# Quarter sums of a DFT matrix in DRAM: eight transfers of 1 MB, or sixteen of 512 KB placed elsewhere

## The chip, the cores and the metric

The kernel runs on one core of a Trainium2 chip. The metric is the device time of one execution in microseconds (us), lower is better; of several timed executions the median is taken.

## What is computed

The reference mixes two branches with a gate per token, all in float32, for 2048 tokens of width 512:

```python
g = sigmoid((x * gate_w).sum(-1, keepdims=True))
a = Cs @ (x @ Cd.T) - Ss @ (x @ Sd.T)      # Real(DFT over tokens of DFT over the width)
b = (silu(x @ w1) * (x @ w3)) @ w2         # SwiGLU, hidden width 1376
out = g * a + (1 - g) * b
```

`Cs`, `Ss` are the real and imaginary 2048x2048 DFT matrices over the tokens (the kernel's input `cc`), `Cd`, `Sd` those of 512x512 over the width (`dd`).

## The kernel before

**Arithmetic.** Every float32 operand is split into a high and a low part (`high`, a copy on ACT, and `low`, a subtraction on DVE), and each product is three matmuls: high by high, high by low, low by high (`mm3`, L124 in the profile). Blocks of 2x2 are multiplied with seven products instead of eight (Strassen-Winograd), so operands are sums of blocks, made on DVE.

**Stages.** In order of time: *gate/up*, L335 to L397, one call `gate_up(n)` per chunk of 128 hidden columns and group of 1024 tokens; then the *transform*, blocks 0 to 3 ("F" blocks, 28 steps each of 12 matmuls, rows of `cc` as the moving operand `zo`); then two blocks of the down projection ("H", moving operand read back from `hsp`), and two of the transform over the width ("Y", from `zsp`). A step loads its operand blocks `B` (`load_c`, L733), sums them on DVE (`sum_c`, L703 and L707), splits them into `zo` (`split_c`, L110 on ACT, L113 on DVE) and multiplies; loads run 8 steps ahead, splits 3. One step of 12 matmuls takes 2.59 us on PE.

**What gate/up moves.** SP loads raw weights `ws` (L224, 512 KB each). ACT and DVE split them to `wa` and, after sums `wu` (L246 to L249), to `wb`. GpSimd's queue (POOL in the profile) stores each `wb` for later use (`wbsp`, L261, 1 MB, two buffers `wb`), and each result `h` in two halves (`hsp`, L324, 256 KB each, three buffers).

**The transform's first block.** Besides the 28 steps, block 0 also loads `xs` (L764, eight of 512 KB), makes from it the second half of the stationary operand (`sum2` on DVE, L178; `high_a2` on ACT, `low_a2` on DVE), and makes the gates: the scores come back from DRAM broadcast to 128 partitions (`s1g<-gs`, L784), ACT applies the sigmoid (L796) and the scalings (L800, L804), and POOL stores them (`gsp`, `ngsp`, L805 and L806). The results of block 0 go to `zsp` by POOL's queue (L933).

**The quarter sums.** The product P1 of blocks 2 and 3 is replaced by one more level of seven products (steps "m1" to "m7", placed among the steps of blocks 1 and 2). Five of them need sums of quarters of `cc`. Four sums are made in DRAM, in the buffer `tsp` of 4 x 2 x 128 x 1024 floats (1 MB for each sum), with no compute engine: a transfer from `cc` (or from an earlier sum) to `tsp`, and an accumulating transfer that adds a second quarter to it. Both go through POOL's queue:

```python
for n, i, b, c in ((0, 1, "b12", "b11"), (1, 3, "b12", "b22"), (2, 2, "T1", "b22"),
                   (3, 4, "T2", "b21")):
    at(0, 3 + 7 * n, quarter_sum, i, b)
    at(0, 6 + 7 * n, lambda i=i, c=c: quarter_sum(i, c, accum_op=ALU.add))
```

`at(blk, n, f)` calls `f` ahead of step `n` of block `blk`, so these eight transfers of 1 MB stand ahead of steps 3, 6, 10, 13, 17, 20, 24 and 27 of block 0. The first read of a sum (`m<-tsp`, L733 on SP) is at 326.1 us.

**What sets the order.** The whole order is written out by hand (`manual_schedule`): each engine and each queue works through its instructions in program order. In gate/up, the tables `early`, `ahead`, `second`, `mid` and `at_end` hold calls for a given `n`; `mid` runs just after the store of `wb`, ahead of the two stores of `h`, and `at_end` after them. An instruction at the head of POOL's queue that waits holds up all behind it.

Of the kernel before, what the change touches and what calls it, by code (L numbers as in the profile page):

```python
# [10 lines left out]
ALU = mybir.AluOpType  # L11
# [22 lines left out]
def fnet_swiglu_gate_kernel(  # L34
# [21 lines left out]
    nc = tc.nc  # L56
# [47 lines left out]
    def free(*tiles):  # L104
        for t in tiles:
            _, places, at = HELD.pop(id(t))
            places.append(at)

    def high(hi, src):
        nc.scalar.activation(hi, src, AF.Copy)  # L110
# [30 lines left out]
    tsp = dram.tile([4, 2, P, 1024], F32, tag="tsp", name="tsp")  # L141
# [63 lines left out]
    def sum_xo(g, k, t):  # L205
        ST[g, k] = t
        nc.vector.tensor_sub(t, *(ST[g, v] for v in SUMS[k]))
# [43 lines left out]
    def wb_parts(w):  # L251
        return flat(WB[w][:, 0]), flat(WB[w][:, 1]), flat(WU[w])

    def high_wb(w):
        WB[w] = wbp.tile([P, 2, 4, 256], F32R, tag="wb", name=f"wb{w}")
        high(wb_parts(w)[0], wb_parts(w)[2])
# [6 lines left out]
    def prod(ps, n, wi, xi, start, chain=False):  # L263
        w = WSET[n]
        w, wi = (WA[w], wi) if wi < 3 else (WB[w], wi - 3)
        x = XO[ITEMS[n][1]]
        for q in range(2):
            sl = slice(q * P, (q + 1) * P)
            mm3(ps, w[:, 0, wi, sl], w[:, 1, wi, sl], x[:, 0, xi, q, :], x[:, 1, xi, q, :],
                start and q == 0, q == 1, chain)  # L270
# [11 lines left out]
    def seed(n, x):  # L282

        y = bank(4 + n % 2, f"Y{n}")
        nc.scalar.activation(y, x, AF.Copy)
        G[n] = (x, y)

    def first2(n):
        prod(G[n][1], n, 1, 1, False, True)
# [26 lines left out]
    def store_h(n, k, h):  # L316

        c, g = ITEMS[n]
        if c == NC - 1:
            nc.gpsimd.dma_start(hlsp[g, :, k * 512 : (k + 1) * 512], h)  # L320
            return
        j = c % NP2
        b = 2 * (c >= NP2)
        nc.gpsimd.dma_start(hsp[g, b + k, j // 2, :, j % 2 * 512 : (j % 2 + 1) * 512], h)  # L324


    early, ahead, second, mid, at_end = {}, {}, {}, {}, {}
# [88 lines left out]
    b12, a21 = zt[0].rearrange("p h a n -> p h (a n)"), zt[1][:, :, 0]  # L416
# [16 lines left out]
    def xo_half(k, q):  # L433
        i = OPS.index(k)
        return XO[0][:, 0, i, q], XO[0][:, 1, i, q], ST[0, k][:, q * 512 : (q + 1) * 512]

    s1 = s1p.tile([P, 512], F32, tag="s1", name="s1_0")
    g1 = u4p.tile([P, 512], F32, tag="u4", name="g1_0")
    h0 = hp.tile([P, 1024], F32, tag="h", name="h0")
# [49 lines left out]
    nc.vector.tensor_mul(h0[:, 512:], g1, C[1, 1])  # L489
    store_h(0, 1, h0[:, 512:])  # L490
    high_wb(1)
    first2(1)
    seed(2, x2)
    low_wb(1)
# [1 line left out]
    gate1(1)  # L496
    sum_xo(0, "T3", ST[0, "B12"])
    sum_xo(0, "T4", ST[0, "B21"])
    first2(2)
    seed(3, x3)  # L500
    for q in range(2):
# [6 lines left out]
    def do(work, n, f, *a):  # L508
        work.setdefault(n, []).append(lambda: f(*a))
# [14 lines left out]
        do(early, n + 3, lambda k=k: low(*xo_parts(1, k)))  # L524
    for n, k in ((7, "B12"), (7, "B11"), (8, "B21"), (9, "B22")):
        do(early, n, lambda k=k: free(ST[1, k]))

    W2R = {}

# [66 lines left out]
    n = NI - 1 - LOOK  # L596
# [35 lines left out]
    for blk, nq in enumerate(NQ):  # L632
        todo_p1 = []
        for n, (k, form, q) in enumerate((k, form, q) for k, form in ORDER[blk] for q in range(nq)):
# [8 lines left out]
            for name in AMONG.get((blk, n), ()):  # L643
                k, h = name[:2], "ab".index(name[2])
# [534 lines left out]
    def at(blk, n, f, *a):  # L1179
        todo.setdefault(NEW[START[blk] + n], []).append((f, a))  # L1180
# [10 lines left out]
    for g, n in enumerate((5, 3)):  # L1191
        for i in range(4):
            at(g, n + i, gates, g, i)
    def quarter_sum(i, b, **kw):


        src = tsp[int(b[1]) - 1] if b[0] == "T" else cc[2 + (b[2] == "2"), 0, 2 * (b[1] == "2") :][:2]
        nc.gpsimd.dma_start(tsp[i - 1], src, max_dma_last_dim=4096, **kw)

    for n, i, b, c in ((0, 1, "b12", "b11"), (1, 3, "b12", "b22"), (2, 2, "T1", "b22"),  # L1200
                       (3, 4, "T2", "b21")):
        at(0, 3 + 7 * n, quarter_sum, i, b)
        at(0, 6 + 7 * n, lambda i=i, c=c: quarter_sum(i, c, accum_op=ALU.add))
    at(1, 12, load_s)
    for i in range(2):
        at(1, 15 + i, sums_s, i)
# [4 lines left out]
    for i, (src, sp, p) in enumerate(late):  # L1211
        blk, n, tag = LATES[i]
# [105 lines left out]
```

## Time and profile before

| | |
|---|---|
| timed executions | 679.31, 675.23, 679.86 us; median 679.31 us |
| the profiled execution's own time | 674.43 us |
| its span, first to last instruction | 672.6 us |
| PE busy | 666.4 us (99%) |
| DVE busy | 589.7 us (88%) |
| ACT busy | 377.3 us (56%) |
| POOL busy (issuing transfers) | 68.2 us (10%) |
| moved by DMA | 185.92 MB, mean 276 GB/s |

The profile is of one execution on the core. "Busy" is the time in which an engine had an instruction; PE is TensorE's matmuls, PEld its weight loads, DVE is VectorE, ACT is ScalarE, POOL is GpSimd, SP the queue that issues most loads. A row of the windows gives, for a stretch of time in us, the busy time of each engine with its number of instructions, the clock that PE was granted (1.00 is full), the mean busy share of the 16 DMA engines, and what they moved in GB/s. A row of the waits names the waiting instruction, what it waited for, the total in us, how often, and the longest. A row of the transfers ends with the median time from issue to landing in us. In rows of time, the number in brackets is the idle time of the engine just before, and what ended it.

### The profile page before, as it was taken

Reading aid. Unit: us, or ns where it says so; the run is one execution under the profiler, and the core shown is the slowest. Engines: PE = TensorE matmul, PEld = TensorE weight load, DVE = VectorE, ACT = ScalarE, POOL = GpSimd, SP = SyncE. Lnnn points to the kernel's source line nnn. Section 1 sums busy time; section 2 is a strip of 40 time slices with the busy share of each in tenths; the row PEclk is TensorE's granted clock in tenths of the full one; section 3 lists DMA queues with packets and bytes.
Section 4 is the critical chain, followed back from the end, with each engine's and each line's share of the span. In section 5 each row is a group of like instructions: output and inputs, shape, how many; then the busy total and the mean of one; then the engine's idle time right before and its main releaser. Section 6 shows DMA issues by size and latency. Waiting matters only on the chain.

```text
span 672.6 us, 8661 instructions
## 1 busy us (share of the span) xinstructions
PE 666.4 (99%) x3089; PEld 577.8 (86%) x3089; DVE 589.7 (88%) x699; ACT 377.3 (56%) x483; POOL 68.2 (10%) x122
## 2 busy tenths in 40 slices
PE   9999999999999999999999999999999999999997
PEld 6888888888888888788888888888888888888887
DVE  6979877787679979979999998999998699799896
ACT  6766556655546864456565664455546447446452
POOL 0011112121111110201000010001100011010000
PEclk9999999999999999999999999999999999999999
DMA  7676655599987999976758557729999969994932
GB/s 296 221 296 229 234 215 210 204 345 378 424 355 256 347 400 256 354 236 217 295 196 323 185 196 288 251 78 338 404 415 295 293 246 356 355 326 178 343 126 94
DMA packets 50683, 185.92 MB, mean 276 GB/s; under 512 B 5840, under 2 KB 7248, under 8 KB 46928
## 3 DMA queue, kind: packets, MB, share of 16 engines
q1 hardware_dynamic: 35872, 125.19, 52.0%
q0 software_dynamic: 14336, 59.52, 24.4%
q10 hardware_dynamic: 432, 0.66, 0.3%
q8 instruction: 24, 0.39, 0.2%
q14 instruction: 19, 0.16, 0.1%
HBM read 130.02 MB, written 63.71 MB: 288 GB/s over the span
## 4 chain that ended last, share of the span: by engine, by line
PE 85%; DMA 7%; issue 4%; DVE 3%; ACT 1%; POOL 1%; SPq 0%; ACTq 0%; DVEq 0%; POOLq 0%
PE P L124 43%; PE X L124 16%; PE quarter L124 12%; PE Z L124 8%; PE Y L124 4%; DMA tsp<-tsp 2%; DMA tsp<-cc 2%; PE C L124 2%; DVE zo L113 1%; DMA s1g<-gs 1%; DMA zsp<-zs 1%; DVE B L703 1%; DMA xs_B<-xt 1%; ACT zo L110 0%; PE V L124 0%
## 5 line engine op out<-in xcount | busy, mean ns | idle before, releaser
L110 ACT ACTIVATE zo<-B 128x1024 fp32r<-128x1024 f32 x178 | 180.4, 1021 | 160.2 <-DVE B L703 74.2
L113 DVE TENSOR_TENSOR zo<-B,zo 128x1024 fp32r<-128x1024 f32 x178 | 208.3, 1178 | 23.2 <-ACT zo L110 22.2
L124 PE MATMUL P<-zo,a 128*128 128x512 f32 x960 | 210.7, 379 | 1.9 <-ACT zu L1048 1.1
L124 PEld LDWEIGHTS P<-zo,a 128*128 128x128 f32 x960 | 181.0, 189 | 29.1 <-DVE zo L113 1.9
L703 DVE TENSOR_TENSOR B<-B,B 128x1024 f32<-128x1024 f32 (+1 forms) x78 | 91.8, 1177 | 0.1
L124 PE MATMUL P<-zo,H 128*128 128x512 f32 x420 | 91.3, 379 | 0.0
L124 PEld LDWEIGHTS P<-zo,H 128*128 128x128 f32 x420 | 79.2, 189 | 11.8 <-issue 0.7
L124 PE MATMUL X<-xo,wb 128*128 128x512 f32 x378 | 88.7, 379 | 0.0
L124 PEld LDWEIGHTS X<-xo,wb 128*128 128x128 f32 x378 | 71.3, 189 | 10.4 <-DVE u L369 0.3
L124 PE MATMUL quarter<-zo,a 128*128 128x512 f32 x324 | 71.9, 379 | 0.0
L124 PE MATMUL P<-zo,Y 128*128 128x512 f32 (+1 forms) x336 | 71.6, 375 | 0.0
L124 PEld LDWEIGHTS P<-zo,Y 128*128 128x128 f32 x336 | 62.6, 189 | 8.7
L124 PEld LDWEIGHTS quarter<-zo,a 128*128 128x128 f32 x324 | 61.2, 189 | 8.7
L324 POOL DMA_DIRECT2D hsp<-h x40 | 21.9, 549 | 112.0 <-DVE h L375 67.2
L386 ACT ACTIVATE h<-X 128x512 f32<-128x512 f32 x21 | 12.5, 596 | 35.3 <-PE X L124 35.3
L124 PE MATMUL Z<-xo,wb 128*128 128x512 f32 x126 | 30.6, 379 | 0.0
L124 PE MATMUL Z<-xo,wa 128*128 128x512 f32 x126 | 30.6, 379 | 0.0
L707 DVE TENSOR_TENSOR B<-B,B 128x1024 f32<-128x1024 f32 (+1 forms) x26 | 30.6, 1177 | 0.0
L124 PE MATMUL X<-xo,wa 128*128 128x512 f32 x126 | 30.5, 379 | 0.0
L124 PE MATMUL Y<-xo,wa 128*128 128x512 f32 x126 | 30.5, 379 | 0.0
L124 PEld LDWEIGHTS Y<-xo,wa 128*128 128x128 f32 x126 | 23.8, 189 | 3.4
L124 PEld LDWEIGHTS Z<-xo,wb 128*128 128x128 f32 x126 | 23.8, 189 | 3.4
(181 smaller groups left out, 660.7 us busy)
## 6 DMA issues: line engine op xcount, KB each, us to landing
B<-cc SPq DMA_DIRECT2D x64, 512.0 KB, 6.2
hsp<-h POOLq DMA_DIRECT2D x40, 256.0 KB, 4.1
wbsp<-wb POOLq DMA_DIRECT2D x8, 1024.0 KB, 4.2
wb<-wbsp SPq DMA_DIRECT2D x8, 1024.0 KB, 8.2
B<-hsp SPq DMA_DIRECT2D x16, 512.0 KB, 8.6
B<-zsp SPq DMA_DIRECT2D x16, 512.0 KB, 8.3
tsp<-cc POOLq DMA_DIRECT2D x6, 1024.0 KB, 11.5
ws<-w SPq DMA_DIRECT2D x11, 512.0 KB, 5.5
```

Of the source, the lines that this page charges most:

```text
L110: nc.scalar.activation(hi, src, AF.Copy)
L113: nc.vector.tensor_sub(lo, src, hi.bitcast(F32))
L124: nc.tensor.matmul(ps.rearrange("p (n a) -> p n a", a=2), u, turns(v)[:, some], **kw)
L324: nc.gpsimd.dma_start(hsp[g, b + k, j // 2, :, j % 2 * 512 : (j % 2 + 1) * 512], h)
L386: nc.scalar.activation(g1, x, AF.Silu)
L703: nc.vector.tensor_add(t, t, RAW[blk, b, q][:, :n])
L707: nc.vector.tensor_sub(t, RAW[blk, "B12", q][:, :n], t)
```

## The change

The same sums are made by sixteen transfers of 512 KB: each sum is worked on in two halves (the second index of `tsp`), copy and accumulation of each half apart. A list `QSUMS` holds them in order (copy of half 0, copy of half 1, accumulation into half 0, accumulation into half 1, for each of the four sums), and each call of `quarter_sum` takes the next. Two calls stand in the straight code ahead of gate/up's loop, nine in `mid` for n = 3, 4, 5, 6, 8, 9, 10, 11, 12, two in `at_end` for n = 6 and 9, three ahead of steps 8, 10 and 12 of the transform's block 1, and none in block 0. Values, layout of `tsp`, queue (POOL) and total bytes are as before.

```diff
+    QSUMS = [(i, b, h) for i, c, d in ((1, "b12", "b11"), (3, "b12", "b22"), (2, "T1", "b22"),
+                                       (4, "T2", "b21")) for b in (c, d) for h in range(2)]
+
+    def quarter_sum():
+        i, b, h = QSUMS.pop(0)
+        src = (tsp[int(b[1]) - 1, h] if b[0] == "T" else
+               cc[2 + (b[2] == "2"), 0, 2 * (b[1] == "2") + h])
+        kw = {"accum_op": ALU.add} if (i, b) in ((1, "b11"), (3, "b22"), (2, "b22"), (4, "b21")) else {}
+        nc.gpsimd.dma_start(tsp[i - 1, h], src, max_dma_last_dim=4096, **kw)
...
     high_wb(1)
+    quarter_sum()
     first2(1)
...
     sum_xo(0, "T4", ST[0, "B21"])
+    quarter_sum()
     first2(2)
...
+    for n in (3, 4, 5, 6, 8, 9, 10, 11, 12):
+        do(mid, n, quarter_sum)
+    for n in (6, 9):
+        do(at_end, n, quarter_sum)
...
-    def quarter_sum(i, b, **kw):
-        src = tsp[int(b[1]) - 1] if b[0] == "T" else cc[2 + (b[2] == "2"), 0, 2 * (b[1] == "2") :][:2]
-        nc.gpsimd.dma_start(tsp[i - 1], src, max_dma_last_dim=4096, **kw)
-
-    for n, i, b, c in ((0, 1, "b12", "b11"), (1, 3, "b12", "b22"), (2, 2, "T1", "b22"),
-                       (3, 4, "T2", "b21")):
-        at(0, 3 + 7 * n, quarter_sum, i, b)
-        at(0, 6 + 7 * n, lambda i=i, c=c: quarter_sum(i, c, accum_op=ALU.add))
+    for n in (8, 10, 12):
+        at(1, n, quarter_sum)
```

The two places where POOL's queue differs follow. In these rows "DMASW" with a number is the completion count of an earlier transfer of this queue (eight counts are used in turn, so a transfer waits at least for the eighth before it), "DVE" and "Activation" are counts of those engines.

POOL's queue in the transform's block 0, before: from the last store of gate/up to the store of the last result of block 0. `tsp` rows are the eight transfers of 1 MB.

```order
L324 DMA hsp_105<-h21_1810 128x512 [waits DMASW5_49,DVE_49]
L1198 DMA tsp_104<-cc 256x1024 [waits DMASW6_49]
L1198 DMA tsp_104<-cc 256x1024 [waits DMASW7_49,DMASW6_49]
L805 DMA gsp_96<-s1g0_1899 128x1024 [waits DMAHW2_49,DMASW0_49,Activation_49]
L806 DMA ngsp_97<-u2g0_1900 128x1024 [waits DMASW1_49]
L1198 DMA tsp_104<-cc 256x1024 [waits DMASW2_49]
L1198 DMA tsp_104<-cc 256x1024 [waits DMASW3_49,DMASW2_49]
L1198 DMA tsp_104<-tsp_104 256x1024 [waits DMASW7_49,DMASW4_49]
L1198 DMA tsp_104<-cc 256x1024 [waits DMASW5_49,DMASW4_49]
L1198 DMA tsp_104<-tsp_104 256x1024 [waits DMASW5_49]
L933 DMA zsp_103<-zu2_0_2157 128x1024 [waits DVE_49]
L933 DMA zsp_103<-zs1_0_2405 128x1024 [waits DMASW0_49,DVE_49]
```

The same place in the changed kernel, on to block 1:

```order
L324 DMA hsp_105<-h21_1823 128x512 [waits DMASW2_49,DVE_49]
L824 DMA gsp_96<-s1g0_1912 128x1024 [waits DMAHW2_49,DMASW3_49,Activation_49]
L825 DMA ngsp_97<-u2g0_1913 128x1024 [waits DMASW4_49]
L952 DMA zsp_103<-zu2_0_2167 128x1024 [waits DMASW5_49,DVE_49]
L952 DMA zsp_103<-zs1_0_2411 128x1024 [waits DMASW6_49,DVE_49]
L952 DMA zsp_103<-zp5_0_2070 128x1024 [waits DMASW7_49,DVE_49]
L952 DMA zsp_103<-zc21_0_2470 128x1024 [waits DMASW0_49,DVE_49]
L824 DMA gsp_96<-s1g1_2494 128x1024 [waits DMAHW5_49,DMASW1_49,Activation_49]
L825 DMA ngsp_97<-u2g1_2495 128x1024 [waits DMASW2_49]
L447 DMA tsp_104<-tsp_104 128x1024 [waits DMASW3_49]
L447 DMA tsp_104<-cc 128x1024 [waits DMASW4_49]
L447 DMA tsp_104<-cc 128x1024 [waits DMASW5_49,DMASW3_49]
```

All `tsp` rows have left block 0: between the last store of gate/up and the gates' second stores stand only stores of gates and results. Three halves follow in block 1, the last an accumulation that waits for the copy two rows above it.

POOL's queue in gate/up before, around n = 4 to 6: for each `wb` one store, for each `h` two.

```order
L261 DMA wbsp_102<-wb5_578 128x2048 [waits DMASW4_49,DVE_49]
L324 DMA hsp_105<-h4_544 128x512 [waits DMASW5_49,DVE_49]
L324 DMA hsp_105<-h4_544 128x512 [waits DMASW6_49,DVE_49]
L261 DMA wbsp_102<-wb6_654 128x2048 [waits DMASW7_49,DVE_49]
L324 DMA hsp_105<-h5_620 128x512 [waits DMASW0_49,DVE_49]
L324 DMA hsp_105<-h5_620 128x512 [waits DMASW1_49,DVE_49]
L261 DMA wbsp_102<-wb7_728 128x2048 [waits DMASW2_49,DVE_49]
L324 DMA hsp_105<-h6_696 128x512 [waits DMASW3_49,DVE_49]
```

The same place in the changed kernel:

```order
L261 DMA wbsp_102<-wb5_581 128x2048 [waits DMASW7_49,DVE_49]
L447 DMA tsp_104<-cc 128x1024 [waits DMASW0_49]
L324 DMA hsp_105<-h4_547 128x512 [waits DMASW1_49,DVE_49]
L324 DMA hsp_105<-h4_547 128x512 [waits DMASW2_49,DVE_49]
L261 DMA wbsp_102<-wb6_658 128x2048 [waits DMASW3_49,DVE_49]
L447 DMA tsp_104<-cc 128x1024 [waits DMASW4_49]
L324 DMA hsp_105<-h5_624 128x512 [waits DMASW5_49,DVE_49]
L324 DMA hsp_105<-h5_624 128x512 [waits DMASW6_49,DVE_49]
L261 DMA wbsp_102<-wb7_733 128x2048 [waits DMASW7_49,DVE_49]
L447 DMA tsp_104<-cc 128x1024 [waits DMASW0_49]
L324 DMA hsp_105<-h6_701 128x512 [waits DMASW1_49,DVE_49]
```

A half of 512 KB now stands between the store of `wb` and the two stores of `h`. No other engine's queue changes its order.

## The prediction

> **What bounds the kernel now.** I read the page's busy times first, then windows by stage, then what PE waits for, then the transfers.
>
> ```profile
> span 672.6 us, 8661 instructions
> PE 666.4 (99%) x3089; PEld 577.8 (86%) x3089; DVE 589.7 (88%) x699; ACT 377.3 (56%) x483; POOL 68.2 (10%) x122
> ```
>
> PE has work in 666.4 of 672.6 us, and the change neither adds nor removes a matmul. All that any edit off PE can win is idle time of PE, 6.2 us in sum. Where it lies:
>
> ```profile
> 0.00:20.00 20.00, 19.12 (x77) 13.88 (x78) 14.79 (x23) 13.32 (x20) 0.89 (x5) 1.00 0.65 249
> 20.00:30.00 10.00, 10.00 (x48) 8.69 (x47) 9.97 (x14) 7.05 (x12) 1.09 (x2) 1.00 0.70 247
> 30.00:40.00 10.00, 10.00 (x48) 8.77 (x47) 7.75 (x13) 7.03 (x10) 1.63 (x3) 1.00 0.95 363
> 40.00:80.00 40.00, 40.00 (x187) 35.03 (x186) 35.11 (x52) 23.47 (x35) 7.60 (x14) 1.00 0.59 228
> 80.00:90.00 10.00, 10.00 (x48) 8.74 (x47) 9.40 (x14) 5.98 (x9) 2.17 (x4) 1.00 0.91 333
> 90.00:130.00 40.00, 40.00 (x187) 35.04 (x186) 29.25 (x51) 22.92 (x37) 7.37 (x13) 1.00 0.48 176
> 130.00:200.00 70.00, 70.00 (x326) 61.01 (x325) 52.09 (x82) 39.19 (x59) 11.73 (x21) 1.00 0.99 382
> 205.00:250.00 45.00, 45.00 (x209) 39.02 (x208) 39.72 (x43) 31.18 (x38) 5.81 (x9) 1.00 0.96 349
> 250.00:275.00 25.00, 23.61 (x108) 20.00 (x108) 25.00 (x26) 13.23 (x14) 1.46 (x2) 1.00 0.97 283
> 275.00:295.00 20.00, 20.00 (x95) 17.50 (x94) 17.28 (x18) 5.92 (x6) 3.12 (x5) 1.00 0.97 302
> 295.00:300.00 5.00, 4.54 (x22) 3.66 (x21) 3.45 (x3) 5.00 (x8) 0.00 (x0) 1.00 0.81 327
> 300.00:320.00 20.00, 20.00 (x94) 17.53 (x93) 19.60 (x22) 13.96 (x18) 3.23 (x6) 1.00 0.58 198
> 600.00:672.00 72.00, 69.17 (x333) 60.70 (x331) 63.13 (x64) 34.40 (x42) 0.72 (x1) 1.00 0.57 204
> ```
>
> The first number after the length is PE, the third DVE, the last two the DMA share and GB/s. PE idles 0.88 us at the start, 2.83 us (and the last 0.6 us) at the end, both outside this change, and in between only in two rows: 25.00 - 23.61 = 1.39 us at 250:275 and 5.00 - 4.54 = 0.46 us at 295:300, **1.85 us together**. Both lie where the DMA share is 0.96 to 1 from 205 on. The clock is 1.00 throughout, so no clock explains them.
>
> The stalls themselves, PE's weight loads and then a matmul, with what ended the wait in brackets:
>
> ```profile
> 251.58 17.78 PEld L124 LDWEIGHTS P<-zo,a 128*128 128x128 f32 x83 [0.69 <-DVE zo L113]
> 270.87 25.98 PEld L124 LDWEIGHTS P<-zo,a 128*128 128x128 f32 x121 [1.51 <-ACT zu L1048]
> 297.71 2.64 PE L124 MATMUL P<-zo,a 128*128 128x512 f32 x11 [0.46 <-DVE zo L113]
> ```
>
> PE waits for DVE and ACT, not for a transfer. But these engines waited for transfers first (waits of 212 to 300 us):
>
> ```profile
> ACT s1g L796 <- DMA s1g<-gs: 5.4, 1, 5.4
> DVE xs L178 <- DMA xs<-xn: 5.0, 6, 2.3
> DVE zo L113 <- ACT zo L110: 4.4, 2, 4.1
> ```
>
> DVE lost 5.0 us to late `xs` loads ahead of 250 us. From 250 to 275 it is busy 25.00 of 25.00 us, catching up, and PE stalls behind it: at 251.58 directly, at 270.87 through ACT, whose `zo` split waits for DVE's sums before its read of the bank (`zu`). The third stall is another chain: the load of scores for the second gates lands late, ACT stands 5.4 us at L796 with the next `zo` behind it, DVE then 4.1 us, PE 0.46 us. And the transfers of 206 to 296 us:
>
> ```profile
> DMA packets 7969, 29.25 MB, mean 325 GB/s; under 512 B 775, under 2 KB 775, under 8 KB 7965
> B<-cc SPq DMA_DIRECT2D x23, 512.0 KB, 10.6
> tsp<-cc POOLq DMA_DIRECT2D x6, 1024.0 KB, 11.5
> xs<-xn SPq DMA_DIRECT2D x8, 512.0 KB, 17.9
> tsp<-tsp POOLq DMA_DIRECT2D x2, 1024.0 KB, 11.3
> s1g<-gs SPq DMA_DIRECT2D x2, 512.0 KB, 10.3
> ```
>
> **What it removes.** Eight transfers of 1.05 MB, 8.4 of the 29.25 MB (29%), leave this stretch; its share falls from about 0.97 to about 0.69 if time goes with bytes (an estimate). At 0.58 in 300:320, the same kind of load lands sooner:
>
> ```profile
> B<-cc SPq DMA_DIRECT2D x6, 512.0 KB, 6.5
> ```
>
> (median of 300 to 345 us, against 10.6). If `xs` gains in the same ratio it lands in 17.9 x 6.5 / 10.6 = 11 us, 7 us earlier, more than the longest single wait of 2.3 us; `s1g` at 10.3 x 0.61 = 6.3 us gains 4 us of the 5.4 that ACT stood, which reaches PE as only 0.46. So DVE's 5.0 us go, and with them the catching-up. DVE's own need does not stand against it: in 205:275 it was busy 39.72 + 25.00 = 64.7 of 70 us, so without the waits it has some 5 us to spare. Gain on PE: all 1.85 us; at least 0 if DVE's backlog stays. I take 1.85.
>
> **What it adds.** Thirteen halves, 6.8 MB, come into 20 to 130 us, where the rows above average a share of 0.62 (0.70 and 0.95 and 0.91 for 10 us each, 0.59 and 0.48 for 40 each). At the 283 GB/s of 250:275 they take 24 us of all engines, 0.22 of 110 us: about 0.84, below full on average, full around 30:40 and 80:90. Three halves in block 1 (300:320, share 0.58) are read only from 326.1 us on. POOL issues sixteen instead of eight, about 0.54 us each as in the row at 59.11 below, on an engine busy 10%.
>
> Two kinds of work could be late in gate/up. Loads of weights, the tightest first:
>
> ```profile
> ws<-w SPq DMA_DIRECT2D x1, 512.0 KB, 7.9
> 30.18 0.33 SPq L224 DMA_DIRECT2D ws<-w  x1
> 39.64 0.84 ACT L110 ACTIVATE wa<-ws 128x768 fp32r<-128x768 f32 x1
> 41.48 0.95 DVE L113 TENSOR_TENSOR wa<-ws,wa 128x768 fp32r<-128x768 f32 x1
> 44.62 0.59 PE L124 MATMUL X<-xo,wa 128*128 128x512 f32 x2
> ```
>
> It lands at 30.18 + 7.9 = 38.1, ACT needs it at 39.64, DVE ends the split at 42.4, PE uses it at 44.62. The two first halves go out at about 22 and 23 us, 1.05 MB or 2.9 us of full transfer at the 363 GB/s of 30:40, partly taken up by 20:30 (0.70). At worst all of it delays this load: 41.0, ACT 1.4 us late, DVE's split done by about 43, PE not late. Cost 0.
>
> And the stores of POOL's queue, now behind or beside a half:
>
> ```profile
> wbsp<-wb POOLq DMA_DIRECT2D x8, 1024.0 KB, 4.2
> 59.11 0.54 POOL L261 DMA_DIRECT2D wbsp<-wb  x1 [5.54 <-DVE wb L113]
> 74.52 1.06 ACT L110 ACTIVATE wb<-wu 128x1024 fp32r<-128x1024 f32 x1 [0.56 <-DVE wu L249]
> 77.00 2.75 PE L124 MATMUL X<-xo,wb 128*128 128x512 f32 x12
> ```
>
> A `wb` stored at 59.11 has landed at 63.3; its buffer is written again at 74.52, a slack of 11.2 us. A half at the block 0 rate of 11.5 us for 1 MB takes 5.8 us: cover enough. `h` has three buffers, so one more call's time. An accumulation waits for a copy issued at least one call of gate/up before it (21 calls fill the 180 us up to 205, 8.6 us each), so it finds a copy of 5.8 us landed. Cost 0; bound from above in the second rival.
>
> The Trainium skill (DMA: Bandwidth & Descriptors, Bandwidth and Anatomy of one DMA) speaks against halves: transfers should be batched to 1 MiB or more, and one issued by GpSimd costs about 2.0 us plus its bytes at 436 GB/s. By that, estimated, sixteen halves of 3.2 us take 51 us where eight of 4.4 us take 35, 16 us more in POOL's queue; but each is also done in 3.2 us, well inside the 11.2 us of slack, so by the page's figure the second rival below could not occur at all. The rows of this case (`wbsp` 4.2 us for 1 MB, `ws` 7.9 us for half of it at a busy time) show that traffic, not size, sets the landing here, so I leave that rival its chance.
>
> **Sum.** 674.43 is the profiled execution's own time; 674.43 - 1.85 + 0 = **672.6 us**. The timed executions' median is 679.31, 4.88 us above it, one of three at 675.23. No trace shows where those 4.88 us lie. PE has slack against DMA everywhere but in block 0, so I expect slower transfers there to make a good part of it (that part goes too), and the rest to stay. Between 672.6 (all goes) and 672.6 + 4.88 = 677.5 (none goes) I take the middle, **675.0 us**.
>
> **Rivals.**
> *Nothing is gained* (chance 0.17). DVE is full in 250:275 in any case and the 1.39 us belong to its own work, the splits for `xs` beside those of the steps. For it: 25.00 of 25.00. Against: the 5.0 us of waits just before. Time: the median as it was, 679.3, or 678.8 with only the 0.46 gone.
>
> *POOL's queue becomes late and gate/up stalls* (0.10), the one on the other side. Five calls of gate/up hold both a `wb` store and a half. If transfers into DRAM with an accumulation hold the queue longer than the rows show, `wb`'s buffer is not free when ACT writes it. PE first reads that `wb` 1.3 us into the row at 77.00 (the row holds two products), and DVE needs 1.2 us after ACT's 1.06, so PE has some 1.5 us left: it decides once the store lands after 74.52 + 1.5 = 76.0, that is 17 us after issue in place of 4.2. At 19 us PE loses 2 us in each of five calls, 10 us; less the 1.85 that is 679.31 + 8.2 = 687.5. At 17.7 us it is 3.5 us, 681.0. Against it: 4.2 to 17 is far.
>
> *All of the 4.88 us was in block 0* (0.13): 672.6, or 1.0% below the median.
>
> My forecast has the remaining 0.60.
>
> **Chances.** About 1% is what a measurement of this kernel can tell from no change, 672.5 to 686.1 us. Faster than that takes the third rival and some scatter to the good side: 0.09. Slower takes the second at its worse half: 0.05. The rest, 0.86, is within. Range: from the third rival, 672.0 with half a microsecond for scatter, past the first (679.3) to the mild end of the second, 681.0.
>
> **What would show it.** Right: `xs<-xn` landing near 11 us and DVE's waits for it under 1 us; PE busy 25.00 of 25.00 in 250:275 and no stall at 297; `ACT s1g` waiting under 1.5 us; DMA share near 0.7 in 205:295 and 0.8 to 0.9 in 20:130; PE still without a gap there. Wrong: a wait of ACT's `wb` or `wa` for a transfer in gate/up that PE follows, `wbsp` landing over 15 us, or the same stalls at 251 and 270 with no wait for `xs` ahead of them. If timed executions stay at 679 while the profile's stalls are gone, their excess lies outside block 0.

## The result, and the profile after

The changed kernel takes **673.48 us** (median of 14 runs, 672.03 to 676.51), the kernel before 676.60 (14 runs, 674.59 to 680.71). The ratio is **0.9948, 95% interval 0.9929 to 0.9968**: some 3 us faster, and inside the 1% that the prediction called the same. The profiled execution itself took 672.55 us, where 674.43 stood before: 1.88 us less, against 1.85 forecast. That agreement is a coincidence, as the stages show.

The span in the page after:

```profile
span 670.8 us, 8667 instructions
```

The windows of the changed kernel, in the columns that the prediction read (PE first after the length, DVE third, DMA share and GB/s last):

```profile
20.00:30.00 10.00, 10.00 (x48) 8.76 (x47) 9.92 (x14) 7.06 (x12) 2.15 (x4) 1.00 0.88 312
30.00:40.00 10.00, 10.00 (x48) 8.74 (x47) 7.75 (x13) 6.67 (x9) 1.63 (x3) 1.00 1.01 398
40.00:80.00 40.00, 40.00 (x187) 35.04 (x186) 35.17 (x52) 23.75 (x35) 10.52 (x18) 1.00 0.82 266
80.00:90.00 10.00, 10.00 (x48) 8.76 (x47) 9.40 (x13) 6.06 (x9) 3.10 (x6) 1.00 1.03 310
90.00:130.00 40.00, 40.00 (x187) 35.01 (x186) 29.24 (x51) 22.91 (x37) 11.71 (x19) 1.00 0.86 276
130.00:200.00 70.00, 68.99 (x320) 59.94 (x319) 50.97 (x80) 39.11 (x59) 11.65 (x21) 1.00 0.99 384
205.00:250.00 45.00, 45.00 (x210) 39.30 (x210) 44.34 (x49) 34.51 (x42) 2.16 (x4) 1.00 0.76 287
250.00:275.00 25.00, 25.00 (x118) 21.89 (x117) 23.86 (x25) 11.20 (x12) 0.53 (x1) 1.00 0.59 208
275.00:295.00 20.00, 20.00 (x94) 17.53 (x93) 18.77 (x19) 11.94 (x14) 1.59 (x3) 1.00 0.51 200
295.00:300.00 5.00, 5.00 (x25) 4.38 (x24) 5.00 (x5) 2.44 (x3) 2.48 (x4) 1.00 0.63 197
300.00:320.00 20.00, 20.00 (x94) 17.51 (x93) 15.76 (x19) 11.56 (x15) 3.07 (x5) 1.00 0.94 282
```

PE has lost its gaps at 250:275 and 295:300. A new one of 70.00 - 68.99 = 1.01 us stands at 130:200, where before it had none. The transfers of 206 to 296 us after:

```profile
xs<-xn SPq DMA_DIRECT2D x8, 512.0 KB, 10.7
s1g<-gs SPq DMA_DIRECT2D x2, 512.0 KB, 7.5
```

The `xs` loads land in 10.7 us instead of 17.9, and in the waits of 212 to 300 us no row of DVE for `xs` and none of ACT for `s1g` is left; the only wait on that path is 1.4 us of ACT for DVE.

The new gap is one stall. Rows of the changed kernel in order of time (start, length, engine and line; in brackets the wait and what ended it):

```profile
128.94 0.64 POOL L447 DMA_DIRECT2D tsp<-tsp  x1
...
131.15 1.14 SPq L551 DMA_DIRECT2D w2r<-w  x1
...
139.70 0.42 DVE L154 TENSOR_TENSOR w2m<-w2r 128x256 f32<-128x256 f32 x1 [2.76 <-DMA w2r<-w]
...
140.96 0.68 DVE L369 TENSOR_TENSOR u<-u,X 128x512 f32<-128x512 f32 x1
...
141.70 2.46 PEld L124 LDWEIGHTS X<-xo,wb 128*128 128x128 f32 x12 [1.41 <-DVE u L369]
```

The same place before, and with it two waits of weight loads behind it that the prediction did not show:

```profile
138.47 0.43 DVE L154 TENSOR_TENSOR w2m<-w2r 128x256 f32<-128x256 f32 x1 [1.61 <-DMA w2r<-w]
...
140.47 2.46 PEld L124 LDWEIGHTS X<-xo,wb 128*128 128x128 f32 x12 [0.26 <-DVE u L369]
248.44 2.46 PEld L124 LDWEIGHTS P<-zo,a 128*128 128x128 f32 x12 [0.39 <-DVE zo L113]
...
297.71 22.31 PEld L124 LDWEIGHTS P<-zo,a 128*128 128x128 f32 x104 [0.86 <-DVE zo L113]
```

The half that call n = 12 issues goes out 2.2 us ahead of the load of the second weights, `w2r`, which lands in 8.5 us instead of 7.4. DVE stands at L154, its sum `u` comes later, and PE needs that sum's bank. The slack was used up before the change already: PE waited 0.26 us there.

How much each stage won or lost follows from where block 0 begins. Its first product in the kernel before:

```profile
206.62 2.75 PE L124 MATMUL P<-zo,a 128*128 128x512 f32 x12
```

and in the changed kernel, with the product ahead of it:

```profile
206.55 1.46 PE L124 MATMUL X<-xo,wb 128*128 128x512 f32 x6
207.85 1.46 PE L124 MATMUL P<-zo,a 128*128 128x512 f32 x6
```

Up to block 0 the change lost 207.85 - 206.62 = **1.23 us** (0.07 of it ahead of the first product, at 5.42 and 5.49 us). From there to the end it takes 670.8 - 207.85 = 462.95 us where before it took 672.6 - 206.62 = 465.98: **3.03 us won**. Net 1.80.

Where the 3.03 us lie, the starts of later products tell. The matmul that comes 419 places after block 0's first begins the first of these rows before, and the second after:

```profile
299.97 0.81 PE L124 MATMUL P<-zo,a 128*128 128x512 f32 x3
298.29 0.81 PE L124 MATMUL P<-zo,a 128*128 128x512 f32 x3
```

These 419 places take 299.97 - 206.62 = 93.35 us before and 298.29 - 207.85 = 90.44 us after: **2.91 us won**, in the stalls of this stretch. The rest is a late stage, where PE's weight loads wait 0.24 and 0.18 us near 582 us in the kernel before and not in the changed one. Block 0's own 28 steps end near 281 us, so the stall at 297 lies in the first steps of block 1; "block 0" below, as in the prediction, stands for 206 to 300 us.

### The profile page after: what moved, and what is told of

Its sections match the earlier page's. It is cut to its first block, busy times and chain, and to the rows that moved or that the text cites. A ratio compares the mean times of both kernels' runs of the same rounds, so it can differ in the third digit from the quotient of the medians.

```text
span 670.8 us, 8667 instructions
## 1 busy us (share of the span) xinstructions
PE 665.4 (99%) x3089; PEld 578.3 (86%) x3089; DVE 589.5 (88%) x699; ACT 378.0 (56%) x483; POOL 73.5 (11%) x130
## 4 chain that ended last, share of the span: by engine, by line
PE 96%; DMA 1%; issue 1%; ACT 0%; DVE 0%; POOL 0%; SPq 0%; POOLq 0%
PE P L124 56%; PE X L124 15%; PE quarter L124 12%; PE Z L124 7%; PE Y L124 4%; PE C L124 2%; DMA hlsp<-h 1%; DMA xs_B<-xt 1%; PE V L124 0%; PE P4left L124 0%; DVE w2b L113 0%; ACT w2b L110 0%; DVE u L369 0%; POOL tsp L447 0%; ACT h L356 0%
```

## The experiments

The theory to test: the whole gain comes from bytes that no longer stand beside the `xs` loads of block 0, and the loss of 1.2 us from the half at n = 12. Its rivals: the halves themselves do it (smaller pieces hold a queue for less time), or POOL's queue does it (in block 0 its own accumulations made it wait, and stores of gates and results stood behind them). A further question was whether block 0 had two chains of stalls, as the prediction had it, or one.

All runs in one table, in three groups of four rows that each share a chip and its runs of the kernel before (medians 674.91, 675.88, 675.80 us). "n = 12" is PE's weight-load stall near 141 us, "block 0" the sum of those of 206 to 300 us; before they are 0.26 and 0.39 + 0.69 + 1.51 + 0.86 = 3.45 us. "419 places" is the time from the start of block 0's first matmul to the start of the one 419 places on, in the profiled execution; before it is 93.35 us.

| kernel | median, us | ratio to before (95%) | span, us | n = 12 | block 0 | 419 places, us |
|---|---|---|---|---|---|---|
| halves_block0 | 678.51 | 1.0058 (1.0033 to 1.0084) | 676.7 | 0 | 3.74 | 95.34 |
| wholes_early | 671.75 | 0.9954 (0.9940 to 0.9967) | 670.0 | 0 | 0 | 90.44 |
| n12_to_block1 | 672.65 | 0.9963 (0.9951 to 0.9976) | 671.1 | 0 | 0 | 90.44 |
| n12_to_end10 | 671.93 | 0.9960 (0.9946 to 0.9974) | 669.5 | 0.20 | 0 | 90.44 |
| two_at_n12 | 675.59 | 1.0000 (0.9985 to 1.0015) | 672.3 | 2.98 | 0 | 90.44 |
| bytes_back | 682.89 | 1.0101 (1.0067 to 1.0135) | 684.8 | 0.76 | 8.27 | 99.86 |
| late_two_block0 | 672.43 | 0.9945 (0.9925 to 0.9964) | 670.6 | 0 | 0 | 90.44 |
| no_sums | 673.68 | 0.9960 (0.9947 to 0.9973) | 670.9 | 0 | 0 | 90.44 |
| change_again | 673.73 | 0.9965 (0.9953 to 0.9978) | 671.4 | 0.85 | 0 | 90.44 |
| end10_again | 672.44 | 0.9948 (0.9934 to 0.9962) | 671.5 | 0.19 | 0 | 90.44 |
| wholes_again | 673.28 | 0.9956 (0.9943 to 0.9969) | 669.9 | 0 | 0 | 90.44 |
| only_first_two | 674.99 | 0.9987 (0.9977 to 0.9998) | 673.5 | 0 | 2.99 | 93.03 |

Without a stall the 419 places take 90.44 us in every kernel. The time over that is what PE lost there: 2.91 us before, 2.59 in only_first_two, 4.90 in halves_block0 and 9.42 in bytes_back (these two with a lower clock after a stall, see the end). The weight loads' waits are another measure: for the four stalls before they exceed the loss by 3.45 - 2.91 = 0.54 us.

### Is it the size of the pieces or their place?

**Halves, but in block 0.** The edit to the changed kernel (the two single calls ahead of the loop go too):

```diff
...
-    for n in (3, 4, 5, 6, 8, 9, 10, 11, 12):
-        do(mid, n, quarter_sum)
-    for n in (6, 9):
-        do(at_end, n, quarter_sum)
...
-    for n in (8, 10, 12):
-        at(1, n, quarter_sum)
+    for n in range(4):
+        for m in (3, 6):
+            for h in range(2):
+                at(0, m + 7 * n, quarter_sum)
```

> Only the halving is kept: the sixteen halves stand in block 0 at the steps of the eight old transfers. Theory A (bytes: the 8.4 MB in block 0 delay the loads of xs and of the scores, whatever their cut): no gain, 676 to 677 us, ratio 0.998 to 1.002; weight-load waits in block 0 of 2 to 4 us as before (3.06). Rival B (halving: finer transfers let the loads through): xs lands well under the 17.9 us of before, waits under 1 us, ratio about 0.995.

Measured: 678.51 us, slower than before. The stalls of block 0 are back, and `xs` lands as late as before. PE's weight loads in this kernel (two waits of 0.29 and 0.24 us lie between these):

```profile
233.67 12.81 PEld L124 LDWEIGHTS P<-zo,a 128*128 128x128 f32 x60 [0.95 <-DVE zo L113]
...
254.19 65.87 PEld L124 LDWEIGHTS P<-zo,a 128*128 128x128 f32 x298 [2.26 <-DVE zo L113]
```

and its `xs` loads of 206 to 296 us:

```profile
xs<-xn SPq DMA_DIRECT2D x8, 512.0 KB, 18.0
```

Halving alone gains nothing, so the rival of the size falls. It came out slower than either theory had it, and the profiled execution shows where: of its 676.7 - 672.6 = 4.1 us, 95.34 - 93.35 = 1.99 lie in block 0, most of them a lower clock after the last stall (see the end), and most of the rest in a stall of a late stage that is 0.24 us before:

```profile
586.58 0.30 PEld L124 LDWEIGHTS V<-ht,wl 128*128 128x128 f32 x2 [2.16 <-ACT V L1097]
```

There ACT stands behind a load of `hl` for 4.28 us, in the kernel before for 2.62. Why that load is later here stays open.

**Wholes, moved.** Eight transfers of 1 MB, at early places like those of the change (`QSUMS` holds eight whole transfers, and one call instead of two stands ahead of the loop):

```diff
...
-        nc.gpsimd.dma_start(tsp[i - 1, h], src, max_dma_last_dim=4096, **kw)
+        nc.gpsimd.dma_start(tsp[i - 1], src, max_dma_last_dim=4096, **kw)
...
-    for n in (3, 4, 5, 6, 8, 9, 10, 11, 12):
+    for n in (4, 6, 8, 9, 11):
         do(mid, n, quarter_sum)
-    for n in (6, 9):
-        do(at_end, n, quarter_sum)
...
-    for n in (8, 10, 12):
+    for n in (8, 12):
         at(1, n, quarter_sum)
```

> Only the move is kept: eight transfers of 1 MB, six of them in gate/up (one ahead of the loop, then n = 4, 6, 8, 9, 11) and two in block 1 (steps 8, 12). None at n = 12. Theory A: no stall in block 0, and without the half at n = 12 none there either, so about 1.3 us better than the change: 672.2 us, ratio 0.993. Rival B: wholes hold up the loads of gate/up, stalls of 1 us or more at n = 4 to 11 that PE follows, ratio 0.996 or more.

Measured: 671.75 us, no stall in block 0 nor at n = 12. Moved wholes are as good as moved halves: the place does it.

### Is it bytes or POOL's queue?

**The bytes put back.** The change, and in block 0 eight plain copies of 1 MB into a spare buffer that nothing reads or waits for:

```diff
...
+    for n in range(8):
+        at(0, 3 + 7 * (n // 2) + 3 * (n % 2),
+           lambda n=n: nc.gpsimd.dma_start(spare[n], cc[2, 0, 2 * (n % 2) :][:2], max_dma_last_dim=4096))
```

> The change plus eight plain copies of 1 MB from cc to a spare buffer in DRAM that nothing reads, at the steps of the eight old transfers, in POOL's queue and waiting for nothing that they do. Theory A (bytes): xs lands at 15 us or later again, weight loads wait 2 us or more in block 0, ratio 0.998 to 1.005. Rival C (what hurt was POOL's queue standing in waits for its own transfers, not the bytes): no stall in block 0, ratio 0.995.

Measured: 682.89 us (the profiled execution, 686.6, is the longest of its five). The stalls come back larger than before, and as in halves_block0 one near 593 us grows too, to 3.23 us. Its weight loads in block 0:

```profile
234.81 12.81 PEld L124 LDWEIGHTS P<-zo,a 128*128 128x128 f32 x60 [1.23 <-DVE zo L113]
...
252.37 2.46 PEld L124 LDWEIGHTS P<-zo,a 128*128 128x128 f32 x12 [2.13 <-DVE zo L113]
259.57 60.48 PEld L124 LDWEIGHTS P<-zo,a 128*128 128x128 f32 x273 [4.75 <-DVE zo L113]
```

and the transfers of 206 to 296 us:

```profile
xs<-xn SPq DMA_DIRECT2D x8, 512.0 KB, 16.7
spare<-cc POOLq DMA_DIRECT2D x8, 1024.0 KB, 13.3
```

In the waits of 212 to 300 us POOL has no row of a wait for one of its own transfers (before: 35.3 us for `tsp<-cc`, 15.1 for `tsp<-tsp`), and `xs` is late all the same; so it is the bytes. It is a heavier dose than before the change, as the first four copies go out in two pairs, so its size is no measure of the gain.

**Two of the four sums back in block 0.** Sums 1 and 3 as halves in gate/up, sums 2 and 4 whole in block 0 at their old steps 17 to 27 (`whole_sum` is the transfer of the kernel before):

```diff
...
-    QSUMS = [(i, b, h) for i, c, d in ((1, "b12", "b11"), (3, "b12", "b22"), (2, "T1", "b22"),
-                                       (4, "T2", "b21")) for b in (c, d) for h in range(2)]
+    QSUMS = [(i, b, h) for i, c, d in ((1, "b12", "b11"), (3, "b12", "b22")) for b in (c, d) for h in range(2)]
...
+    for n, i, b, c in ((2, 2, "T1", "b22"), (3, 4, "T2", "b21")):
+        at(0, 3 + 7 * n, whole_sum, i, b)
+        at(0, 6 + 7 * n, lambda i=i, c=c: whole_sum(i, c, accum_op=ALU.add))
```

> Sums 1 and 3 as halves in gate/up as in the change; sums 2 and 4 as four transfers of 1 MB in block 0 at their old steps (17, 20, 24, 27). The prediction had two chains: xs loads (up to 250 us), then the load of the second scores (286 us). If so, the stalls near 251 and 271 go, and the one at 297 stays with about 0.9 us; none at n = 12. Span about 670.3, ratio 0.994. If block 0's stalls are one chain of backlog, all or none of them stay.

Measured: 672.43 us, no stall in block 0 at all. Half of the transfers in block 0 cost nothing, even with this DMA share:

```profile
205.00:250.00 45.00, 45.00 (x210) 39.31 (x209) 44.58 (x49) 33.79 (x41) 3.67 (x6) 1.00 0.93 332
```

Its first `xs` loads and its first whole transfer, in order of time (SPq is SP's queue):

```profile
211.02 7.12 SPq L782 DMA_DIRECT2D xs<-xn  x5
...
231.10 0.57 POOL L1216 DMA_DIRECT2D tsp<-tsp  x1
```

In the kernel before, the first copy went out just ahead of these loads, and its accumulation when it had landed:

```profile
209.17 0.58 POOL L1198 DMA_DIRECT2D tsp<-cc  x1
222.73 0.95 POOL L1198 DMA_DIRECT2D tsp<-cc  x1 [12.98 <-DMA tsp<-cc]
```

So the mean share of 45 us does not decide. The first six `xs` loads, issued from 211 to 221.5 us, go out with none of these transfers under way; the last two, at 234.27 and 236.52, go out with one under way, and DVE waits for none of the eight. `xs` lands in 11.4 us here, near the 10.7 with all sums moved. The stall of 0.9 us at 297 that this run was to show, the second chain of the prediction, did not come.

**The other two alone.** The kernel before without sums 2 and 4 (the steps that need them read a quarter of `cc`):

```diff
...
-    for n, i, b, c in ((0, 1, "b12", "b11"), (1, 3, "b12", "b22"), (2, 2, "T1", "b22"),
-                       (3, 4, "T2", "b21")):
+    for n, i, b, c in ((0, 1, "b12", "b11"), (1, 3, "b12", "b22")):
```

> The kernel before with sums 1 and 3 only, at their old steps 3, 6, 10 and 13 of block 0; sums 2 and 4 are left out, and the steps that need them read a quarter of cc. The converse of the run with the last two sums in block 0, which had no stall there. If one backlog made by late xs loads is the cause: xs lands at 16 us or more, DVE waits 4 us or more for it, and stalls of 1 us or more remain near 251; the one at 271 remains in part, the one at 297 not, as nothing delays the scores. Span 670.5 to 671.5. If it were the sum of all eight transfers: no stall, 669.5.

Measured: 674.99 us; three of the four stalls are there, the one at 271 (here 272.68) whole and not in part. The span of 673.5 us lies above the range, 1.5 us of it ahead of block 0: the first product starts at 6.95 us here and at 5.42 before.

```profile
250.25 2.46 PEld L124 LDWEIGHTS P<-zo,a 128*128 128x128 f32 x12 [0.79 <-DVE zo L113]
253.39 17.78 PEld L124 LDWEIGHTS P<-zo,a 128*128 128x128 f32 x83 [0.69 <-DVE zo L113]
272.68 47.35 PEld L124 LDWEIGHTS P<-zo,a 128*128 128x128 f32 x220 [1.51 <-ACT zu L1048]
```

with DVE's wait of 212 to 300 us behind them:

```profile
DVE xs L178 <- DMA xs<-xn: 4.9, 4, 2.7
```

The first two sums alone make the stalls up to 273 us, the last two alone make none. The stall at 297 came with neither half alone, so it is no chain of its own. The second load of `s1g` shows how both halves enter: it goes out at 285.71 us and lands in 8.6 before, at 282.48 and in 5.5 with the first two sums, at 276.76 and in 5.3 with the last two. The backlog of the first two delays its issue, the traffic of the last two its landing: the eighth transfer of 1 MB, which the list of POOL's queue ahead of the prediction ends too early to show, goes out at 283.57 us, 2.1 us ahead of it. (halves_block0 has 285.06 and 8.6 and no stall there; its PE is 2.2 us later by then.)

### The half at n = 12

**A dose series**: that half left out of gate/up, moved to the end of call 10, and doubled.

```diff
-    for n in (3, 4, 5, 6, 8, 9, 10, 11, 12):
+    for n in (3, 4, 5, 6, 8, 9, 10, 11):
         do(mid, n, quarter_sum)
...
-    for n in (8, 10, 12):
+    for n in (6, 8, 10, 12):
         at(1, n, quarter_sum)
```

> The change with the one half of n = 12 moved to step 6 of block 1 (four there). If the stall of 1.41 us at 141.7 us comes from that half, which holds back the load of w2r behind it (A): that stall is gone, span 669.5, time 1.2 to 1.4 us under the change's 673.5, so 672.2 us, ratio 0.993. If the load of w2r is late for another reason (D): the stall stays and the time is the change's, ratio 0.995; a fourth half in block 1 could also cost there, seen as a wait of PE at 295 to 320.

```diff
-    for n in (3, 4, 5, 6, 8, 9, 10, 11, 12):
+    for n in (3, 4, 5, 6, 8, 9, 10, 11):
         do(mid, n, quarter_sum)
-    for n in (6, 9):
+    for n in (6, 9, 10):
         do(at_end, n, quarter_sum)
```

> The change with one more half at the end of n = 10, so that all later ones come one place earlier and none is left at n = 12. A: as for the move to block 1, no stall at 141.7, ratio 0.993, with POOL waiting 2 to 4 us at n = 11 for the accumulation it copies from, which costs nothing. D: stall stays, ratio 0.995.

```diff
-    for n in (3, 4, 5, 6, 8, 9, 10, 11, 12):
+    for n in (3, 4, 5, 6, 8, 9, 10, 11, 12, 12):
         do(mid, n, quarter_sum)
...
-    for n in (8, 10, 12):
+    for n in (10, 12):
         at(1, n, quarter_sum)
```

> The change with a second half at n = 12, taken from step 8 of block 1: the dose doubled. A: the load of w2r lands one more half later (1.1 us more, as the first half cost it 7.4 to 8.5 us), the stall at 141.7 us grows from 1.4 to about 2.5 us or more, time 674.7 us, ratio 0.9965. D: stall unchanged near 1.4, ratio 0.995.

Measured, from the landing of `w2r` to PE:

| kernel | halves at n = 12 | `w2r` lands in, us | DVE waits, us | PE stalls, us |
|---|---|---|---|---|
| n12_to_block1 | 0 | 6.4 | 0.6 | 0 |
| n12_to_end10 | 0 | 7.3 | 1.6 | 0.20 |
| before | 0 | 7.4 | 1.6 | 0.26 |
| change_again | 1 | 8.0 | 2.2 | 0.85 |
| the change | 1 | 8.5 | 2.8 | 1.41 |
| two_at_n12 | 2 | 10.1 | 4.3 | 2.98 |

The last row's stall, in the kernel with two halves:

```profile
143.18 2.46 PEld L124 LDWEIGHTS X<-xo,wb 128*128 128x128 f32 x12 [2.98 <-DVE u L369]
```

Past 1.4 us of DVE's wait each further microsecond reaches PE whole: 2.8 - 1.41, 2.2 - 0.85 and 4.3 - 2.98 are all 1.3 to 1.4. That settles the cause of the loss: one half ahead of `w2r` costs PE 0.6 to 1.2 us over the kernel before, two cost 2.7. The times go the same way, 672.65 and 671.93 us without that half and 675.59 with two, though against their own runs of the kernel before the ratios (0.9963, 0.9960, 1.0000) are higher than forecast (0.993, 0.993, 0.9965). Here as in block 0 the harm of a transfer is the load that it stands before.

### What is left, and the better version

**The sums left out altogether**: the changed kernel without all sixteen halves (the steps that need the sums read a quarter of `cc`).

> The sums are not made at all; the steps that need them read a quarter of cc instead. No stall is left in block 0 nor at n = 12: the floor for any placing, span about 669.4, ratio 0.992 to 0.993. If it is no better than the change (0.995), the change's stall at 141.7 has another cause; if it is better than the two moves of n = 12, their transfers still cost something.

Measured: 673.68 us, not less than the kernels that move the sums, and no better than the change, which was to mean that the stall at 141.7 has another cause. Its profile says otherwise: there is no stall at n = 12 nor in block 0, and from the first product to block 0 it takes 201.08 us, where n12_to_end10 takes 201.19, wholes_early 201.18 and the change 202.36. So in these executions the two moves came within about 0.1 us of a kernel without the sums up to there, and to nothing over it in block 0. What hides it in the time are two stalls in a later stage, which neither of the first two profiles shows:

```profile
559.93 3.75 PEld L124 LDWEIGHTS P<-zo,H 128*128 128x128 f32 x18 [0.42 <-DVE zo L113]
564.55 15.19 PEld L124 LDWEIGHTS P<-zo,H 128*128 128x128 f32 x71 [0.87 <-DVE zo L113]
```

They stand in n12_to_block1, late_two_block0, change_again and end10_again too (0.51 to 0.77 and 0.87 us), and not in wholes_early, wholes_again, n12_to_end10 or only_first_two. They come without any sum, so the sums don't cause them. DVE stands just before them at its own L154:

```profile
556.80 0.42 DVE L154 TENSOR_TENSOR c21p<-s1p 128x256 f32<-128x256 f32 x1 [1.53 <-DMA nbsp<-zc]
```

The store `nbsp<-zc` that it waits for lands in 9.1 to 9.4 us in the five kernels with these stalls, and in 6.1 to 7.6 in the nine others. Why it takes longer in some executions stays open. The stalls blur every difference of about 1 us.

**The change and the two better placings on one chip**, the kernels as above:

> The change itself once more, beside the two next kernels on one chip. Its half at n = 12 should show the stall of about 1.4 us near 141.7 us again; ratio 0.995 to 0.998.

> The change with one more half at the end of n = 10 and none at n = 12, again. If the stall at n = 12 is worth its 1.4 us (A), 0.8 to 1.4 us under the change on the same chip, ratio 0.001 to 0.002 lower. If other stalls take its place (the waits near 560 us that some profiles show): no difference to the change.

> Eight whole transfers moved out of block 0, none at n = 12, again. If halving is worth nothing: as the kernel beside it with the halves and none at n = 12, within 0.5 us. If wholes hold up gate/up: slower than it.

Measured: 673.73, 672.44 and 673.28 us against 675.80 before. With that half at the end of call 10 the kernel is 1.3 us faster than the change by these medians, as expected; moved wholes are 0.45 faster, 0.84 and not 0.5 from the kernel beside them. The intervals (0.9953 to 0.9978, 0.9934 to 0.9962, 0.9943 to 0.9969) overlap, so the order is not settled. Nor are the moved sums always free in gate/up: end10_again has waits of 0.24 and 0.57 us near 160 us, the second for a read of `wbsp`, and takes 202.04 us from the first product to block 0, against 201.19 for the same kernel as n12_to_end10; smaller ones for `wbsp` (0.18 to 0.35 us) stand in n12_to_block1, n12_to_end10 and wholes_again. Either placing will do, about 0.4 to 0.5% under the kernel before.

## Why the prediction was right, step by step

It gave 675.0 us, range 672.0 to 681.0, most chance to "within 1%"; measured were 673.48 us and a ratio of 0.9948. The profiled execution's 672.6 us came out by luck, through two errors of opposite sign; the main mechanism was right.

- **The mechanism of block 0: right.** Late `xs` loads, then DVE's backlog, then PE. `xs` was to land near 11 us and lands in 10.7; DVE's waits are gone; PE is busy 25.00 of 25.00 us at 250:275. The share of 205:295 was to be 0.69 and is (0.76 x 45 + 0.59 x 25 + 0.51 x 20) / 90 = 0.66. The rival "nothing is gained" falls: DVE is at 44.34 of 45 us in 205:250 after the change, so it does its work there on time instead of in 250:275. That other copies' bytes beside the `xs` loads were the cause is shown from both sides, by bytes_back, which puts them back, and by late_two_block0, which keeps them away from the first loads alone.
- **The gain of 1.85 us: too small**, measured 2.91 in block 0. The step that failed is "PE idles only in two rows". A matmul's record is longer than its place in the stream: six are put at 1.46 us while the next six begin 1.30 us after them (206.55 and 207.85 above), so 0.16 us of every stall counts as busy, and a short stall (0.39 us at 248.44) does not show. By the starts in the trace, the second matmul after each stall also begins 0.32 us after the first, where 0.22 is usual. Four stalls hide 4 x (0.16 + 0.10) = 1.04 us in this way, and 1.85 + 1.04 = 2.89. The bracketed waits of the weight loads err the other way, 3.45 us for the same four. The Trainium skill (Perfetto Trace Analysis, Identifying the Most-Contended Engine) calls matmul busy time a poor measure of how close a kernel is to its peak, because matmuls are pipelined, and has the weight loads' busy time looked at; this trace agrees that the busy time misleads, with 1.85 of 2.91 us. The prediction also put the DMA share at "0.96 to 1 from 205 on", which its row of 295:300 (0.81) does not show.
- **Two chains: wrong, without harm to the sum.** The score load `s1g` was read as a second cause, late only in landing. late_two_block0 has late traffic and no stall, only_first_two the stalls without the one at 297; and the load went out 285.71 - 278.06 = 7.7 us later before than after, held up by the backlog. `s1g` lands in 7.5 us, not in the 6.3 estimated, and nothing waits for it.
- **Gate/up at cost 0: wrong**, measured (207.85 - 5.49) - (206.62 - 5.42) = 1.16 us from the first product to block 0. The load `ws` at 30.18, which the prediction took as the tightest, came out as worked out: ACT was 1.05 us late (1.4 at worst was forecast) and PE was not. `wbsp` lands in 5.5 us instead of 4.2 and stays far inside its 11.2 us of slack. The share, 0.84 forecast, is (8.8 + 10.1 + 32.8 + 10.3 + 34.4) / 110 = 0.88. What failed is "two kinds of work could be late": there is a third, the loads of the second weights, and their slack was nil (PE's 0.26 us of wait above). The tightest load was picked from the start of the stage, where the first halves go out, and not searched for behind each of the sixteen. Also the test "PE still without a gap there" ended at 130 us, where the last half goes out; its damage is 12 us later.
- **Block 1 at cost 0: right**: at 300:320 the share is 0.94 and PE 20.00 of 20.00.
- **POOL's queue as the losing case: did not occur.** A copy of half a megabyte takes 9.1 us in gate/up (median of ten of 20 to 130 us), above the 5.8 estimated and far under the 17 us from which a store would have been late. The estimate of 3.2 us by the Trainium skill (DMA: Bandwidth & Descriptors, Anatomy of one DMA) is far under the 9.1 us measured beside this traffic. Its rule to batch to 1 MiB or more (Bandwidth) made no difference that could be told: 671.93 us with halves and 671.75 with wholes in one group, 672.44 and 673.28 in the other.
- **The 4.88 us of the timed runs: mis-sized.** Over 14 runs the kernel before is 676.60 - 674.43 = 2.2 us above its profiled execution, not 4.88; after the change it is 673.48 - 672.55 = 0.9. So 0.9 us stood where the prediction put 2.4, and this is why 675.0 was 1.5 us too high. A median of three runs carried that error. That some of the excess went is not shown: each figure is the distance of a median from one execution, and the executions of a kernel differ by 4 to 6 us. So the third rival, that all of the excess was block 0's, has neither its size nor its time. Other profiles show three places outside block 0 where executions differ: the start of the first product (5.40 to 6.95 us), the two stalls near 560 us, and the one near 582 us (593 in bytes_back).

## What to carry to other kernels

Before moving background transfers, list every just-in-time load that goes out within one landing time behind each new place, with the slack of its reader; one such load without slack cost 1.16 of the 2.91 us won here. The harm of a copy depends on which loads it stands before, hardly on its size or on the mean share of the stage, so only the copies in front of tight loads need to move. Measure what PE's stalls cost by the starts of the same matmuls in two profiles: here its busy time showed too little (1.85 of 2.91 us) and the waits of its weight loads too much (3.45).

## What the runs showed of the hardware

After some stalls PE's granted clock fell. It was one stretch at half speed each time: in 2 us windows from 254 us halves_block0 shows 0.70, 0.50 and 0.95, which is (0.30 + 0.50 + 0.05) x 2 / 0.5 = 3.4 us at 0.50. The trace's own record of the clock has 3.413 us for this stretch and for two in bytes_back, and the time at full speed between those two is 331.09 us, 97 times as long. So these changes fall on a grid of 3.41 us. The rows of halves_block0 on its grid (PE and the weight loads are the first two times after the length, the clock stands before the DMA share):

```profile
251.38:254.80 3.42, 1.56 (x8) 1.06 (x7) 2.23 (x3) 1.72 (x2) 0.00 (x0) 1.00 1.07 267
254.80:258.21 3.41, 3.41 (x10) 2.66 (x9) 3.41 (x5) 1.13 (x2) 0.00 (x0) 0.50 1.00 335
258.21:261.62 3.41, 3.41 (x18) 2.98 (x17) 3.41 (x4) 2.13 (x2) 0.90 (x2) 1.00 0.64 226
```

In the stretch at half speed 8 matmuls begin and in the next one 16, so the stall is followed by another 8 x 0.216 = 1.7 us of loss. In two_at_n12, after a longer stall than that of halves_block0 (2.98 against 2.26 us on the weight loads), the clock stayed; on the grid of that execution:

```profile
141.29:144.70 3.41, 1.51 (x7) 1.33 (x8) 3.31 (x7) 1.95 (x3) 0.00 (x0) 1.00 1.00 409
144.70:148.11 3.41, 3.41 (x18) 2.98 (x17) 3.24 (x6) 2.86 (x5) 1.09 (x2) 1.00 0.74 187
```

This stall began at about 140.2 us, so the edge of the grid at 141.29 cut it in two. The length of a single stall does not decide it, then. In the three windows just ahead of a fall the weight loads were busy 1.06 us (halves_block0), 0.30 and 1.08 us (bytes_back). In windows cut by a stall with 1.33 us (two_at_n12) and 1.18 us (bytes_back, 249.63 to 253.05) the clock stayed. What counts seems to be how much of a stall falls into one window; no limit follows, as the clock also stayed after the window from 4.77 to 8.18 us of only_first_two, with 0.79 us. Four of the ten executions of two_at_n12 have a mean clock of 0.997, and they are its four longest (675.78 to 677.52 us); whether the same stall met the grid otherwise in them is not shown. The Trainium skill (TensorE: Matmul & The Clock Gate, Part 1: The HAM clock gate) gives a window of about 3.4 us that runs freely, and half speed after one idle window. The length and the grid agree; a window that is idle throughout was not needed here, as PE had 1.06 us of weight loads in the one of halves_block0.
